# Fused attention and two MoE layers: unread products in early PE gaps, three key tiles in the accumulator, GpSimd taken from the first splits, an early sigmoid table, new order constants

## The chip, the cores and the metric

One core of a Trainium2 chip. The metric is the device time of the whole program in microseconds (us), median of several runs. The names used are those of the profile: PE is TensorE, DVE VectorE, ACT ScalarE, POOL GpSimd, SP the engine whose queue issues DMAs.

## The reference

```
scores = q k^T / 8, kept where the key is one of 4 sinks or within a window of 128, else -1e9
a = softmax(scores); x = (a v), heads put side by side          # 2 x 768 tokens, 8 heads of 64, so 1536 x 512
h = x @ w_in; g = h if h >= 1, 0 if h <= -1, else (h + 1)^2 / 4; x = g @ w_out          # d_ff 2048
gate = sigmoid(x @ w_gate); val = x @ w_val; out = (gate * val) @ w_out2                # d_ff 1536
```

The weights are float64 in memory and are passed as pairs of 32-bit words.

## The kernel before, in words

**Attention.** Each of the two batches is cut in seven query tiles of 112 tokens (the last has 96), numbered t = 0 to 13 over both; each tile has four head pairs. For a pair: PE multiplies queries and keys (scores, L873, 64 rows of the array at a time), DVE scales, masks and takes the extreme of a row (`top`, L876, two for a pair), ACT takes the exponential and sums (L882), PE transposes (L890), ACT or DVE copies the transposes out of PSUM (`pts`), PE multiplies by the values (L913, 64 columns at a time, the four pairs of a tile together). At a tile's end the sums are inverted (L927, L928, DVE), widened to `ie`, spread by four transposes (L936), and the output `on` is copied, multiplied (L947) and split in two fp32r parts, `xh` (a copy) and `xl` (a difference).

**MoE.** Every product runs on such split parts, three matmuls for one (L515 to L517 for w_in, L560 to L562 for w_out, L671 for the gate and value layer, which forms blocks from seven products of sums). The first block of 512 tokens can start when the first five tiles (t = 0 to 4) are split. Weights are decoded from float64 words: a DMA into `st`, then `rebase` on ACT (L418), `clamp` and `shift` (L421, L424), `sign` and `tail` (L427, L430) on DVE, then `halves` splits the result into the tiles `early` or `late`: a copy (L324, L326 or L328 on ACT, DVE or POOL) and a difference (L331 on DVE or POOL).

**The order.** Nothing runs in the order of the code. Every piece is given to `Plan.op` with its engine or the engines it may go to, a cost for each, a due time and what it reads and writes. `Plan.order` walks through time with these costs, picks for each free engine the piece that is due first (`SAME_MODE` prefers, on PE, the mode of 64 rows, 64 columns or the full array that it is in), and chooses engine and PSUM bank; the instructions are issued in that order. Each engine, and SP's queue of DMAs, then runs its list in order and waits on semaphores. The constants at the file's head (`FINISH`, `EARLY`, `LATE`, `BIAS`, ...) move due times.

**The start.** Before a branch that tests the sizes, keys and queries of tile 0 are loaded into the then unused accumulator `acc`, its values behind them, both from SP; six unread matmuls run on PE (L1158). Keys of later tiles go to `qk` buffers with two places for each pair; an even and an odd tile lie side by side, which is why tile 1 needs tile 0's block loaded a second time.

Of the kernel before, what the change touches and what calls it, by code (L numbers as in the profile page):

```python
# [54 lines left out]
BIAS = {"DVE": 0.02, "POOL": -0.14, "ACT": -0.17}  # L55

SLOT_DUE = 2.54

FINISH = {"top": 1.49, "exp": 7.0, "turn": 1.26, "pts": 2.81, "values": -0.74, "div": 3.95, "out": 4.29}
MOE_DUE = 63.45  # L60
MOE_PACE = 3.48
DRAIN = 3.77
EARLY = 11.77
LATE = 18.92
# [5 lines left out]
SAME_MODE = 1.11  # L70
WARM = 6

# [9 lines left out]
def a_us(n):  # L82
    return 0.093 + n / 1200
# [14 lines left out]
def g2_us(n):  # L98
    return 0.15 + n / 476
# [34 lines left out]
class Plan:  # L134
# [130 lines left out]
    def run(self):  # L265
        order, end = self.order()
        for o in order:
            for b in o.new:
                b.ap = b.ring.make(b.bank if b.ring.banks else b.at % b.ring.n)
            o.fn(o.eng) if o.pick else o.fn()  # L270
        return end


class Body:
# [46 lines left out]

    def copy(self, e, out, x):
# [53 lines left out]
    def halves(self, x, n, hi, lo, hk, lk, due, reads, after=()):  # L376
# [27 lines left out]
    def raw(self, src, due):  # L404
# [12 lines left out]
        def rebase():  # L417
            nc.scalar.activation(out=w.ap, in_=high().bitcast(F32), func=AF.Copy, scale=REBASE)  # L418
# [14 lines left out]
        op("ACT", a_us(512), due, rebase, [st], [w])  # L433
# [6 lines left out]
    def load(self, nm, i, due):  # L440
# [8 lines left out]
        def split(x, c, n, reads):  # L449
            self.halves(x, n, lambda: self.at(h, c, n), lambda: self.at(l, c, n), self.held(h, c, n), self.held(l, c, n), due, reads, after)  # L450
# [138 lines left out]


# [191 lines left out]
    def moe(self, first):  # L782

        rest = []
# [11 lines left out]
    def banded(self):  # L796
# [25 lines left out]
        def slot(k, due):  # L822
# [3 lines left out]
            mask = masks.of(i)  # L826

            ks = 1 if i == 0 else 2
            at = i % 2
# [5 lines left out]
            src = lambda j: self.a["qk"][b, j, p]  # L835
            if t == 0:
                c0, *there = pre["raw"][p]
                own, v = (lambda: there[0]), (lambda: there[1])
                rq, rv = cells("acc", 0, c0, c0 + NQK), cells("acc", 0, c0 + NQK, c0 + NQK + P)
                op("SP", 0.0, -99.0, lambda: None, [], rq, lat=0.0)  # L840
                op("SP", 0.0, -99.0, lambda: None, [], rv, lat=2.0 + 0.2 * p)
            else:
                v_b = Buf(v_r)
                own, v = (lambda: block(p, at)), (lambda: v_b.ap)
                rq, rv = [mine, before] if i else [mine], [v_b]
# [12 lines left out]
            def keys(es):  # L858

                x = kept[p][es]  # L860
                if at:
# [58 lines left out]
            if p == NP - 1:  # L920
# [23 lines left out]
                op({"ACT": a_us(NP * P), "DVE": d1_us(NP * P), "POOL": g1_us(NP * P)}, 0, due - FINISH["div"], widen, [sm], [ie])  # L944
# [3 lines left out]
                op({"ACT": a_us(m), "DVE": d1_us(m), "POOL": g1_us(m)}, 0, due - FINISH["out"], lambda e: self.copy(e, xh, y()), [on], xhk)  # L948
                self.att_end = op({"DVE": d2_us(m), "POOL": g2_us(m)}, 0, due - FINISH["out"], lambda e: self.less(e, xl, y(), f32v(xh)), [on] + xhk, xlk)
# [119 lines left out]
class Masks:  # L1069
# [20 lines left out]
    def of(self, i):  # L1090
        return (self.first, self.second, self.even, self.odd)[min(i, 2 + i % 2)]
# [28 lines left out]
def moe_chain_kernel(ctx: ExitStack, tc: tile.TileContext, a, out):  # L1120
# [12 lines left out]
    with tc.manual_schedule():  # L1133
# [5 lines left out]
        for p in range(min(KD, NP)):  # L1139
            c0 = p * NT + S  # L1140
            qk = pre["acc"][:, c0:c0 + NQK]
# [98 lines left out]
```

## Time and profile before

| | |
|---|---|
| time, median of 3 runs | 641.52 us (641.24 to 641.83) |
| time of the profiled execution | 640.57 us |
| its span, first to last instruction | 638.8 us |
| PE busy, share of the span | 624.0 us, 98% |
| DVE, ACT, POOL busy | 518.8, 316.2, 81.8 us |
| TensorE clock, mean granted | 0.994 |
| PE busy before 52.1 us, where the first MoE product starts | 44.17 us |
| PE idle in 345 to 372 us | 1.50 us |
| PE idle in 625 to 638.8 us | 5.40 us |

Idle time before the first MoE product (7.93 us), in the one gap near 370 us and at the end make up nearly all that PE is not busy in. A busy PE can still be at half clock.

### The profile page before, as it was taken

How to read it: one execution, taken by the hardware profiler on the slowest of the kernel's cores; microseconds unless marked ns; L12 is line 12 of the kernel's file. 1: busy time of each engine (PE TensorE's matmuls, PEld its weight loads, DVE VectorE, ACT ScalarE, POOL GpSimd, SP SyncE). 2: the span in 40 equal slices, each digit the busy share in tenths (PEclk: the TensorE clock that was granted, in tenths of full speed). 3: DMA queues.
4: the chain of work that ended last, by engine and by line, in shares of the span. 5: the costliest groups of instructions: out<-in, count | busy, mean ns of one | idle time of the engine just before them, and what ended most of it. 6: DMA issues, size and time to landing. Idle time of an engine off the chain costs nothing.

```text
span 638.8 us, 9816 instructions
## 1 busy us (share of the span) xinstructions
PE 624.0 (98%) x3514; PEld 540.4 (85%) x3514; DVE 518.8 (81%) x1136; ACT 316.2 (50%) x723; POOL 81.8 (13%) x95
## 2 busy tenths in 40 slices
PE   8979999999999999999999999999999999999996
PEld 5667788888888888888888889999999998999995
DVE  4899999699999885456979598799887899786373
ACT  4989988655533521232535376554352353433330
POOL 0022200020100120010102111122120021120000
PEclk8999999999999999999999999999999999999999
DMA  6666665122534130000310003322211222200004
GB/s 189 208 199 207 202 188 197 51 72 94 165 107 129 62 99 34 0 1 13 120 34 1 1 0 100 100 66 67 72 61 34 100 94 72 67 0 1 2 34 170
DMA packets 28571, 54.48 MB, mean 85 GB/s; under 512 B 3296, under 2 KB 18400, under 8 KB 28512
## 3 DMA queue, kind: packets, MB, share of 16 engines
q1 hardware_dynamic: 28512, 53.75, 25.8%
q8 instruction: 30, 0.49, 0.3%
q14 instruction: 29, 0.24, 0.1%
HBM read 50.60 MB, written 3.15 MB: 84 GB/s over the span
## 4 chain that ended last, share of the span: by engine, by line
PE 92%; DVE 3%; ACT 3%; issue 0%; DMA 0%; POOL 0%; DVEq 0%; ACTq 0%
PE bank L671 27%; PE bank L515 7%; PE bank L560 7%; PE bank L517 7%; PE bank L516 7%; PE bank L562 7%; PE bank L561 7%; PE bank L758 5%; PE bank L759 5%; PE bank L757 5%; PE bank L873 3%; PE bank L913 3%; PE bank L890 2%; DVE pr L876 1%; ACT pr L882 1%; PE bank L936 1%
## 5 line engine op out<-in xcount | busy, mean ns | idle before, releaser
L671 PE MATMUL bank<-xh,early 128*128 128x384 f32 x384 | 107.7, 335 | 1.5 <-ACT bank L324 1.5
L671 PE MATMUL bank<-late,early 128*128 128x384 f32 x432 | 85.2, 335 | 0.0
L671 PEld LDWEIGHTS bank<-late,early 128*128 128x128 f32 x432 | 76.0, 188 | 0.6
L671 PEld LDWEIGHTS bank<-xh,early 128*128 128x128 f32 x384 | 70.2, 188 | 2.4 <-ACT bank L324 2.1
L324 ACT ACTIVATE early<-w 128x512 fp32r<-128x512 f32 (+1 forms) x46 | 26.2, 572 | 86.0 <-PE bank L671 32.9
L671 PE MATMUL bank<-xl,early 128*128 128x384 f32 x192 | 64.3, 335 | 0.0
L767 DVE TENSOR_TENSOR acc<-bank,acc 128x512 f32<-128x512 f32 (+1 forms) x61 | 41.4, 679 | 26.4 <-PE bank L759 26.3
L882 ACT ACTIVATE pr<-pr,mx 112x256 f32<-112x256 f32 (+2 forms) x112 | 54.0, 488 | 9.3 <-DVE mx L876 9.0
L418 ACT ACTIVATE w<-st 128x512 f32<-128x512 f32 x68 | 44.9, 668 | 15.2 <-DMA st<-in_w 9.4
L534 ACT ACTIVATE tmp<-tmp 128x512 f32<-128x512 f32 x48 | 30.1, 630 | 42.8 <-DVE tmp L531 42.5
L427 DVE SCALAR_TENSOR_TENSOR w<-st,w 128x512 int32<-128x512 int32 x68 | 46.8, 691 | 0.5
L430 DVE SCALAR_TENSOR_TENSOR w<-st,w 128x512 int32<-128x512 int32 x68 | 46.7, 689 | 0.4
L531 DVE TENSOR_SCALAR tmp<-bank 128x512 f32<-128x512 f32 x48 | 32.7, 685 | 17.1 <-PE bank L517 16.8
L576 DVE TENSOR_TENSOR acc<-bank,acc 128x512 f32<-128x512 f32 x36 | 24.1, 687 | 23.5 <-PE bank L562 23.4
L876 DVE CUSTOM_DVE_ANT_0 pr<-bank,mask 112x256 f32<-112x256 f32 (+2 forms) x112 | 39.4, 394 | 4.5 <-PE bank L873 4.5
L324 ACT ACTIVATE gs<-tmp 128x512 fp32r<-128x512 f32 (+1 forms) x49 | 30.4, 621 | 23.6 <-DVE tmp L537 21.7
L331 DVE TENSOR_TENSOR gs<-tmp,gs 128x512 fp32r<-128x512 f32 (+1 forms) x51 | 34.4, 678 | 5.5 <-ACT gs L324 5.0
L515 PE MATMUL bank<-xh,early 128*128 128x512 f32 x96 | 38.8, 404 | 0.0
L560 PE MATMUL bank<-gs,early 128*128 128x512 f32 x96 | 38.2, 398 | 0.0
L517 PE MATMUL bank<-xh,early 128*128 128x512 f32 x96 | 37.5, 391 | 0.0
L516 PE MATMUL bank<-xl,early 128*128 128x512 f32 x96 | 37.5, 390 | 0.0
L562 PE MATMUL bank<-gs,early 128*128 128x512 f32 x96 | 37.4, 390 | 0.0
(170 smaller groups left out, 1498.3 us busy)
## 6 DMA issues: line engine op xcount, KB each, us to landing
st<-in_w SPq DMA_DIRECT2D x32, 512.0 KB, 3.4
qk<-in_qk SPq DMA_DIRECT2D x56, 128.0 KB, 3.0
v<-in_vb SPq DMA_DIRECT2D x52, 128.0 KB, 3.3
st<-in_wg SPq DMA_DIRECT2D x12, 512.0 KB, 3.3
st<-in_wv SPq DMA_DIRECT2D x12, 512.0 KB, 3.3
st<-in_wo SPq DMA_DIRECT2D x12, 512.0 KB, 3.3
out<-acc SPq DMA_DIRECT2D x11, 256.0 KB, 2.3
acc<-in_qk SPq DMA_DIRECT2D x4, 128.0 KB, 2.8
```

Source lines behind the costliest of these rows:

```text
L324: self.nc.scalar.activation(out=out, in_=x, func=AF.Copy)
L418: nc.scalar.activation(out=w.ap, in_=high().bitcast(F32), func=AF.Copy, scale=REBASE)
L427: nc.vector.scalar_tensor_tensor(out=t(), in0=high(), scalar=-0x80000000, in1=t(), op0=ALU.bitwise_and, op1=ALU.bitwise_or)
L430: nc.vector.scalar_tensor_tensor(out=t(), in0=low(), scalar=29, in1=t(), op0=ALU.logical_shift_right, op1=ALU.bitwise_or)
L515: mm(out=out, lhsT=wh[:, c], rhs=mh, start=k == 0, stop=False)
L516: mm(out=out, lhsT=wh[:, c], rhs=ml, start=False, stop=False)
L517: mm(out=out, lhsT=wl[:, c], rhs=mh, start=False, stop=k == KD - 1)
L560: mm(out=out, lhsT=wh[:, c], rhs=gh, start=f == fs[0], stop=False)
L562: mm(out=out, lhsT=wl[:, c], rhs=gh, start=False, stop=f == fs[-1])
L671: nc.tensor.matmul(out=out, lhsT=w[:, c], rhs=m, start=start and i == n == 0, stop=i == 1 and n == 2, skip_group_check=True)
L876: nc.vector.tensor_tensor_reduce(out=pr.ap[:n, e, :ks * P], in0=banks[e].ap[:n, j, :ks * P], in1=mask[:n, :ks * P], op0=ALU.add, op1=ALU.m ...
L882: nc.scalar.activation(out=pr.ap[:n, e, :ks * P], in_=pr.ap[:n, e, :ks * P], func=AF.Exp, bias=mx.ap[:n, e:e + 1], scale=-1.0, accum_out=s ...
```

## The change

- `fillers` and `fill`: where the plan leaves PE idle for more than 0.32 (in the plan's units) in the first 55, fp32 products of the 128 x 128 identity by itself are put in, into a PSUM bank that is free then; nobody reads them.
- `RAW` = 3: keys and queries of the tiles 0, 1 and 2 lie in `acc`, side by side, so the block of tile 0 isn't loaded again for tile 1; the `qk` buffers begin at tile 3, where tile 2's block is loaded a second time. The values of tile 0 are loaded from ACT's queue.
- `some`, `pool`, `POOL_FROM` = 5: the splits of the first eight weight pieces, and for the tiles 0 to 4 `widen` and the split of the output, may no longer go to POOL.
- `raw`: `rebase` of the first eight weight pieces may go to POOL as well as to ACT.
- `table`: a sigmoid of one element on ACT behind the attention's last split.
- Constants of the order, `SAME_MODE` from 1.11 to 3.41 among them.

```diff
-FINISH = {"top": 1.49, "exp": 7.0, "turn": 1.26, "pts": 2.81, "values": -0.74, "div": 3.95, "out": 4.29}
+FINISH = {"top": 0.74, "exp": 7.79, "turn": 6.83, "pts": 5.29, "values": -2.39, "div": 3.03, "out": -3.93}
...
-SAME_MODE = 1.11
+SAME_MODE = 3.41
 WARM = 6
+RAW = 3
+POOL_FROM = 5
+FILL, FILL_US, FILL_MIN = 55.0, 0.22, 0.1
...
+    def fillers(self, order, banks):
+        spans = [[] for _ in banks]
+        for b in {b for o in self.ops for b in o.bufs if b.bank is not None}:
+            spans[b.bank].append((min(u.start for u in b.users), max(u.end for u in b.users)))
+        todo, last = {}, 0.0
+        for o in order:
+            if o.eng != "PE":
+                continue
+            n = int((o.start - last - FILL_MIN) / FILL_US)
+            if o.start < FILL and n > 0:
+                free = [i for i, s in enumerate(spans) if all(z < last or a > o.start for a, z in s)]
+                if free:
+                    todo[o] = n, free[0]
+            last = o.start + o.on["PE"]
+        return todo
...
+    def fill(self, n, bank):
+        for _ in range(n):
+            self.nc.tensor.matmul(out=self.psum[bank][:, :P], lhsT=self.pre["ident"], rhs=self.pre["ident"], start=True, stop=True)
...
+    def some(self, pool, **on):
+        return {e: t for e, t in on.items() if pool or e != "POOL"}
...
-        hp = self.plan.op({"ACT": a_us(n), "DVE": d1_us(n), "POOL": g1_us(n)}, 0, due, lambda e: self.copy(e, hi(), x()), reads, hk, after=after)
-        lp = self.plan.op({"DVE": d2_us(n), "POOL": g2_us(n)}, 0, due, lambda e: self.less(e, lo(), x(), f32v(hi())), [*reads, *hk], lk, after=after)
+        hp = self.plan.op(self.some(pool, ACT=a_us(n), DVE=d1_us(n), POOL=g1_us(n)), 0, due, lambda e: self.copy(e, hi(), x()), reads, hk, after=after, port=True)
+        lp = self.plan.op(self.some(pool, DVE=d2_us(n), POOL=g2_us(n)), 0, due, lambda e: self.less(e, lo(), x(), f32v(hi())), [*reads, *hk], lk, after=after, port=True)
...
-        op("ACT", a_us(512), due, rebase, [st], [w])
+        op({"ACT": a_us(512), "POOL": g1_us(512)} if self.asked < 2 * STAGES[0] else {"ACT": a_us(512)}, 0, due, rebase, [st], [w])
...
+        x = self.pre["scratch"]
+        self.plan.op("ACT", 1.5, self.due, lambda: self.nc.scalar.activation(out=x, in_=x, func=AF.Sigmoid), after=[self.att_end])
...
+            if t < RAW:
+                c0, first = pre["raw"][p]
+                held = lambda j: cells("acc", 0, c0 + j * NQK, c0 + (j + 1) * NQK)
+                own = lambda: pre["acc"][:, c0 + t * NQK:c0 + (t + 1) * NQK]
+                rq = [k for j in (t - 1, t) if j >= 0 for k in held(j)]
+            else:
+                own, rq = (lambda: block(p, at)), [mine, before] if i else [mine]
...
-                if t == 1:
-                    load(lambda: block(p, 0), src(0), due - 6, [before])
-                load(own, src(i), due - 6, [mine])
+                if t == RAW:
+                    load(lambda: block(p, 1 - at), src(i - 1), due - 6, [before])
+                load(own, src(i), due - 6, held(t) if t < RAW else [mine])
...
-                op({"ACT": a_us(NP * P), "DVE": d1_us(NP * P), "POOL": g1_us(NP * P)}, 0, due - FINISH["div"], widen, [sm], [ie])
+                pool = t >= POOL_FROM
+                op(self.some(pool, ACT=a_us(NP * P), DVE=d1_us(NP * P), POOL=g1_us(NP * P)), 0, due - FINISH["div"], widen, [sm], [ie], port=True)
...
-            nc.sync.dma_start(out=v, in_=a["vb"][0, 0, p, :, 1])
+            nc.scalar.dma_start(out=v, in_=a["vb"][0, 0, p, :, 1])
```

What this makes of the order is shown at three places. Names: `bank` is a PSUM bank, `pr` the exponentials, `ident` the identity, `st` and `w` a weight as loaded and as decoded.

PE between the scores of tile 0 and the values of tile 0, before:

```order
L890 MATMUL bank_164<-ident,pr 128x112 x2
L890 MATMUL bank_165<-ident,pr 128x112 x2
L873 MATMUL bank_158<-qk_175 112x256
L873 MATMUL bank_159<-qk_175 112x256
L873 MATMUL bank_158<-qk_179 112x256
L873 MATMUL bank_159<-qk_179 112x256
L936 MATMUL bank_162<-ident,ie 128x112 x4
L913 MATMUL bank_160<-pts,acc 64x112 x8
```

and of the change (L349 is a product that nobody reads, L922 scores, L939 transposes):

```order
L349 MATMUL bank_163<-ident 128x128 x5
L939 MATMUL bank_162<-ident,pr 128x112 x2
L349 MATMUL bank_158<-ident 128x128
L939 MATMUL bank_163<-ident,pr 128x112 x2
L349 MATMUL bank_158<-ident 128x128 x4
L922 MATMUL bank_164<-acc 112x256
L922 MATMUL bank_165<-acc 112x256
L922 MATMUL bank_164<-acc 112x256
L922 MATMUL bank_165<-acc 112x256
L939 MATMUL bank_158<-ident,pr 128x112 x2
L939 MATMUL bank_159<-ident,pr 128x112 x2
L349 MATMUL bank_161<-ident 128x128 x2
```

Ten unread products now stand ahead of tile 1's first scores, those scores have moved ahead of the last two pairs' transposes of tile 0, and they read `acc`. Up to the first MoE product there are 29 such products. The last scores of tile 2 stand behind the spread of tile 1 before, and ahead of it in the change.

POOL from the branch on, before:

```order
L328 TENSOR_SCALAR xh<-on 128x4x112 x2
L328 TENSOR_SCALAR early<-w 128x512
L328 TENSOR_SCALAR ie<-sm 112x512
L331 TENSOR_TENSOR early<-w,early 128x512 x2
L328 TENSOR_SCALAR ie<-sm 112x512 x2
L328 TENSOR_SCALAR early<-w 128x512
L331 TENSOR_TENSOR early<-w,early 128x512
L331 TENSOR_TENSOR xl<-on,xh 128x4x112
```

and of the change (L453 is `rebase`, L357 a copy, L360 a difference):

```order
L453 TENSOR_SCALAR w<-st 128x512 x4
L357 TENSOR_SCALAR ie<-sm 112x512
L453 TENSOR_SCALAR w<-st 128x512 x2
L357 TENSOR_SCALAR xh<-on 128x4x112
L453 TENSOR_SCALAR w<-st 128x512 x2
L360 TENSOR_TENSOR gs<-tmp,gs 128x512
L357 TENSOR_SCALAR ie<-sm 112x512
L360 TENSOR_TENSOR xl<-on,xh 128x4x112
```

All eight rebases have gone to POOL, and the differences that stood third on its list have gone to DVE.

ACT where the first gates are formed, before:

```order
L324 ACTIVATE gs<-w 128x512
L324 ACTIVATE tmp<-bank_165 128x384
L324 ACTIVATE late<-acc 128x384
L712 ACT_TABLE_LOAD
L712 ACTIVATE rest<-bank_158 128x384
L324 ACTIVATE xh<-rest 128x384
L324 ACTIVATE late<-tmp 128x384
L324 ACTIVATE bank_161<-bank_160 128x384
```

and of the change:

```order
L353 ACTIVATE late<-acc 128x384
L451 ACTIVATE w<-st 128x512
L353 ACTIVATE xh<-rest 128x384
L753 ACTIVATE rest<-bank_164 128x384
L353 ACTIVATE tmp<-bank_165 128x384
L353 ACTIVATE bank_160<-bank_158 128x384
```

The load of the sigmoid's table (L712 before) is no longer among these; it stands behind the attention's last split on ACT's list.

## Rows read from the trace of the kernel before

**Rows 1.** The page: PE's busy time, and its clock in 40 slices.

```profile
PE 624.0 (98%) x3514; PEld 540.4 (85%) x3514; DVE 518.8 (81%) x1136; ACT 316.2 (50%) x723; POOL 81.8 (13%) x95
...
PEclk8999999999999999999999999999999999999999
```

**Rows 2.** Stretches: PE, PEld, DVE, ACT, POOL busy; PE clock, DMA share, GB/s.

```profile
0.00:52.10 52.10, 44.17 (x380) 32.19 (x381) 41.45 (x167) 39.32 (x130) 7.70 (x21) 0.93 0.63 198
...
52.10:130.00 77.90, 77.90 (x688) 63.29 (x687) 71.35 (x232) 65.82 (x199) 8.66 (x11) 1.00 0.52 163
...
9.90:16.30 6.40, 6.40 (x36) 4.23 (x36) 2.79 (x14) 3.20 (x11) 0.00 (x0) 0.50 0.84 252
...
37.00:46.00 9.00, 6.26 (x66) 4.58 (x66) 8.90 (x31) 6.62 (x22) 1.58 (x2) 1.00 0.65 228
```

**Rows 3.** Who waited for whom: us in total, times, longest.

```profile
PE bank L936 <- POOL ie L328: 2.1, 3, 1.4
...
PE bank L671 <- ACT bank L324: 1.5, 1, 1.5
...
ACT pr L882 <- DVE mx L876: 9.0, 4, 4.6
```

**Rows 4.** Timeline of DVE: start, us, instruction, idle before it and its releaser.

```profile
12.73 0.42 DVE L876 CUSTOM_DVE_ANT_0 pr<-bank,mask 112x256 f32<-112x256 f32 x1 [1.58 <-PE bank L873]
...
15.95 0.62 DVE L947 TENSOR_TENSOR on<-on,bank 128x448 f32<-128x448 f32 x1 [1.76 <-ACT on L324]
...
17.62 0.42 DVE L876 CUSTOM_DVE_ANT_0 pr<-bank,mask 112x256 f32<-112x256 f32 x1 [0.51 <-PE bank L873]
...
23.52 0.42 DVE L876 CUSTOM_DVE_ANT_0 pr<-bank,mask 112x256 f32<-112x256 f32 x1 [1.74 <-PE bank L873]
...
24.90 0.76 DVE L421 TENSOR_SCALAR w<-w 128x512 f32<-128x512 f32 x2
...
34.95 3.50 DVE L331 TENSOR_TENSOR xl<-on,xh 128x448 fp32r<-128x448 f32 x1
...
44.51 0.72 DVE L331 TENSOR_TENSOR xl<-on,xh 128x448 fp32r<-128x448 f32 x1
```

**Rows 5.** Timeline of POOL.

```profile
35.47 2.49 POOL L331 TENSOR_TENSOR early<-w,early 128x512 fp32r<-128x512 f32 x2
44.13 0.62 POOL L328 TENSOR_SCALAR ie<-sm 112x512 f32<-112x512 f32 x1 [6.17 <-DVE sm L928]
```

**Rows 6.** The chain that ended last: start, us, engine, tile, line.

```profile
18.05 0.54 DVE xl L331
...
28.39 0.34 DVE ie L326
...
40.01 0.54 DVE pts L326
...
41.23 0.34 DVE pr L876
...
63.15 1.05 PE bank L873 x8
...
81.65 1.91 PE bank L873 x16
```

**Rows 7.** Timeline of PE: the unread products before the branch.

```profile
1.73 2.93 PE L1158 MATMUL warm<-ident 128*128 128x128 f32 x12 [1.73 <-POOL ident masks.py:199]
```

**Rows 8.** SP's queue, and DMA issues of the first 20 us with time to landing.

```profile
13.57 0.90 SPq L415 DMA_DIRECT2D st<-in_w  x2
...
st<-in_w SPq DMA_DIRECT2D x3, 512.0 KB, 4.8
```

**Rows 9.** Timeline of ACT, and of PE, at the first gates.

```profile
367.74 1.28 ACT L712 ACT_TABLE_LOAD   x1
369.04 0.49 ACT L712 ACTIVATE rest<-bank 128x384 f32<-128x384 f32 x1
...
370.79 0.44 PE L671 MATMUL bank<-xh,early 128*128 128x384 f32 x1 [1.50 <-ACT bank L324]
```

More of the change, by code (lines that the diff above doesn't have):

```diff
@@ L53 @@
 START = {"DVE": 0.9}
-BIAS = {"DVE": 0.02, "POOL": -0.14, "ACT": -0.17}
-SLOT_DUE = 2.54
-FINISH = {"top": 1.49, "exp": 7.0, "turn": 1.26, "pts": 2.81, "values": -0.74, "div": 3.95, "out": 4.29}
[L60 to L64, printed above, removed]
+BIAS = {"DVE": 0.32, "POOL": -0.16, "ACT": -0.15}
+SLOT_DUE = 2.58
+FINISH = {"top": 0.74, "exp": 7.79, "turn": 6.83, "pts": 5.29, "values": -2.39, "div": 3.03, "out": -3.93}
+MOE_DUE = 65.99
+MOE_PACE = 3.5
+DRAIN = 2.46
+EARLY = 10.7
+LATE = 23.51
 ENTER, LEAVE = {"rows": 0.18, "cols": 0.14}, 0.09
@@ L263, in order, with run @@
         return order, now
-    def run(self):
+    def fillers(self, order, banks):
[13 more added lines that the diff above has]
+        return todo
+    def run(self, banks=(), fill=None):
         order, end = self.order()
+        todo = self.fillers(order, banks) if fill else {}
         for o in order:
+            if o in todo:
+                fill(*todo[o])
             for b in o.new:
@@ L415, in dma, with rebase @@
             nc.sync.dma_start(out=st.ap.rearrange("p n t -> p (n t)"), in_=src.bitcast(I32))
-        def rebase():
-            nc.scalar.activation(out=w.ap, in_=high().bitcast(F32), func=AF.Copy, scale=REBASE)
+        def rebase(e):
+            if e == "ACT":
+                nc.scalar.activation(out=w.ap, in_=high().bitcast(F32), func=AF.Copy, scale=REBASE)
+            else:
+                nc.gpsimd.tensor_scalar(out=w.ap, in0=high().bitcast(F32), scalar1=REBASE, scalar2=1.0, op0=ALU.mult, op1=ALU.mult)
         def clamp():
@@ L449, in split @@
         def split(x, c, n, reads):
-            self.halves(x, n, lambda: self.at(h, c, n), lambda: self.at(l, c, n), self.held(h, c, n), self.held(l, c, n), due, reads, after)
+            self.halves(x, n, lambda: self.at(h, c, n), lambda: self.at(l, c, n), self.held(h, c, n), self.held(l, c, n), due, reads, after, self.asked >= 2 * STAGES[0])
         if nm not in PAIR_AT:
@@ L588, in block, with table @@
         after(3, t)
+    def table(self):
+        x = self.pre["scratch"]
+        self.plan.op("ACT", 1.5, self.due, lambda: self.nc.scalar.activation(out=x, in_=x, func=AF.Sigmoid), after=[self.att_end])
     def quarters(self, b):
@@ L782, in moe @@
     def moe(self, first):
+        if first:
+            self.table()
         rest = []
@@ L947, in slot @@
                 op("DVE", d2_us(m), due - FINISH["div"], lambda: nc.vector.tensor_tensor(out=y(), in0=y(), in1=ib.ap[:, :, :n], op=ALU.mult), [ib], [on])
-                op({"ACT": a_us(m), "DVE": d1_us(m), "POOL": g1_us(m)}, 0, due - FINISH["out"], lambda e: self.copy(e, xh, y()), [on], xhk)
-                self.att_end = op({"DVE": d2_us(m), "POOL": g2_us(m)}, 0, due - FINISH["out"], lambda e: self.less(e, xl, y(), f32v(xh)), [on] + xhk, xlk)
+                op(self.some(pool, ACT=a_us(m), DVE=d1_us(m), POOL=g1_us(m)), 0, due - FINISH["out"], lambda e: self.copy(e, xh, y()), [on], xhk, port=True)
+                self.att_end = op(self.some(pool, DVE=d2_us(m), POOL=g2_us(m)), 0, due - FINISH["out"], lambda e: self.less(e, xl, y(), f32v(xh)), [on] + xhk, xlk, port=True)
             yield None
@@ L1166, in moe_chain_kernel @@
             body.moe(1)
-            body.plan.run()
+            body.plan.run(body.banks, body.fill)
     with branch.Else():
```

33 lines of the change are left out of this document (16 added, 17 removed).

## The prediction

> **What bounds the kernel now.** I read the page first. PE is busy for 98% of the span and its clock is full in 39 of 40 slices [rows 1], so time can come back only where PE stands, where its clock is low, or where its list gets shorter. The table of stretches finds these places: up to 52.1 us, where the first MoE product starts, PE is busy for 44.17 us, so it stands 7.93; from there to 130 us it is busy throughout [rows 2]. The waits add one place, 1.5 us behind ACT at the first gates [rows 3, 9]. The rest of PE's idle time lies at the end (front table), which the change doesn't touch. So the end comes when the first MoE product starts, plus what PE's list then takes: a microsecond that the first five tiles gain early is a microsecond of the total, as long as PE stays full afterwards.
>
> What holds the first product back, then? Three things. From 9.9 to 16.3 us PE is busy all the time at a clock of 0.50 [rows 2], the lower of its two levels, 1.2 GHz; before that it had stood between short transposes. DVE waits in this stretch and behind it four times, 1.58, 1.76, 0.51 and 1.74 us [rows 4]. And at 34.95 us a difference that usually delays the next DVE instruction by 0.54 [rows 6] takes 3.50 [rows 4], while GpSimd works on two differences for 2.49 [rows 5]; around it PE is busy for only 6.26 us of 9.00 and DVE for 8.90 [rows 2]. From about 25 us on DVE is full, and what its list holds up to tile 4's split decides.
>
> **The change part by part.** The profiled execution took 640.57 us, 0.95 below the median of 641.52; the sum is made against 640.57 and carried over to the median. A difference of under 0.2%, 1.28 us, is about what this measurement cannot tell from none.
>
> *Unread products.* Six of them took 2.93 us before the branch [rows 7], at the low clock by my reading, 0.49 each; half of it, 0.24, at the high one. Ten of them stand between tile 0's scores and tile 1's, 2.4 us in a place where PE only had four pairs of transposes and waited for exponentials. If that keeps the clock up, the 6.40 us of work at 0.50 [rows 2] take 3.2: a gain of 3.2, taken out of DVE's first three waits, which sum to 3.85 [rows 4]. Bounds: 0, if the clock falls anyway, and 3.85. I take 3.2, since DVE stood exactly behind PE's slow scores and values. One product stands ahead of tile 0's scores: +0.49 at the low clock (bounds 0 and 0.49). The 17 later ones lie in gaps of the plan; where a gap is not there they cost 17 x 0.24 = 4.1, which is the far bound; I take 0, because PE has idle time of 2.74 us in 37 to 46 alone [rows 2] and DVE, not PE, is behind.
>
> *The order of scores.* The fourth wait of 1.74 is for scores of tile 2 that stood on PE's list behind a spread, which itself waited for DVE. They now stand ahead of the spread: -1.74 (bounds 0 and -1.74).
>
> *Keys in the accumulator.* Tile 1 needs four loads fewer, but the queue of SP now issues the keys of tile 3, twice the count for that tile, ahead of the first weights: the first `st` is the 23rd DMA behind the branch instead of the 17th. It was issued at 13.57, two issues take 0.90, so six more put it at about 16.3, and with 4.8 us to landing [rows 8] it is there at 21.1. GpSimd's rebase takes 0.62, by the copy of 512 elements for each partition in rows 5: ready at 21.7. DVE came to its first clamp at 24.90 [rows 4]; less the 4.9 of waits, with the 0.49, and 0.2 for a reshuffled list (four more `top`, less three copies, by the 0.34 and 0.54 of [rows 6]) it comes at 20.7. So it now waits 1.0 there, and behind the clamp on DVE's list queue the last `top` of tile 3 and the division of tile 1, for which ACT and PE wait. Bounds: 0 and 2.2 (a landing one microsecond later). The four loads of tile 0's values sit on ACT's list ahead of its first table load; ACT waits up to 4.6 us for its first exponential [rows 3], which covers four issues of 0.45. Without that cover they would cost 1.8.
>
> *First splits without GpSimd.* The stall goes: 3.50 - 0.54 = -2.96. DVE's list up to the fifth `xl` changes, counted in the two orders: one cast of a weight and one of `xh` more (0.34 and about 0.30), two differences of weights more (0.54 for 448 elements gives 0.62 for 512, so 1.24), four `top` of tile 5 more (4 x 0.34 = 1.36), and six `pts` copies fewer, two of them half as wide (4 x 0.54 + 2 x 0.27 = 2.70): +0.54. The rebases go off ACT, which is busy for 39.32 of 52.1 us [rows 2] and so not first in line; it takes over the copies and two widenings.
>
> *What the sum doesn't see.* DVE, ACT and PE now all end their lists for tile 4 within a few microseconds of each other, and small waits between them remain. Bounds 0 and 2.74, PE's idle time in 37 to 46 [rows 2]; I take 1.0, below the middle, because in that stretch DVE was busy for 8.90 of 9.00.
>
> So the first product starts at 52.1 - 3.2 + 0.49 - 1.74 + 1.0 - 2.96 + 0.54 + 1.0 = 47.2, 4.9 us earlier.
>
> *After it.* PE's groups of scores behind the first product fall from ten to seven. Two groups apart cost 2 x 1.05, together 1.91 [rows 6]: 0.19 for each, -0.57 (bounds 0 and -0.57). DVE is busy for 71.35 of 77.9 us up to 130 and ACT for 65.82 [rows 2], so the table load of 1.28, now at the attention's end, has 12 us of ACT's idle time to lie in, and costs nothing; if PE had to wait for it there, 1.28. Five differences of `xl` go to GpSimd behind the first product: nothing, or some stalls as below.
>
> *The gates.* ACT loads the sigmoid's table for 1.28 us in front of the first gate, and PE waits 1.50 for a copy that stands behind it [rows 9]. Without the load the copy comes 1.28 earlier: -1.28 (bounds 0, if the new list of ACT, which puts a rebase there, is as late, and -1.50). By the Trainium skill, ScalarE: Activation LUTs, "What ACT_TABLE_LOAD costs", a change of set costs a drain of about 1.38 us beside the 1.28, 2.66 in all. The trace agrees with the 1.28; the next sigmoid starts 0.02 us behind the load [rows 9], so no drain shows behind it, and by the page the gain would still be no more than the 1.50 that PE waits.
>
> Sum: -4.9 - 0.57 - 1.28 = -6.8, or 633.8 for the profiled execution and **634.7** for the median.
>
> **The rivals.** *GpSimd holds DVE again.* The stalled difference of 3.50 [rows 4] shows that DVE can be held for as long as GpSimd works. Five rebases of 0.62 each run before the first product now; if each holds a DVE instruction for its whole time, that is 3.1, and the time 637.8. Against it: beside a copy of 0.62 on GpSimd at 44.13 [rows 5] the difference at 44.51 took 0.72 [rows 4], longer by 0.1 to 0.2 and not 0.62, and before the change there were about as many such copies in this stretch. The Trainium skill, GPSIMD Engine Reference, "Key points", says that GpSimd shares its SBUF interfaces with VectorE, with contention where a VectorE instruction runs in a 2-port mode or has two SBUF inputs. The 3.50 agrees with it, and the clamp, shift and sign behind each rebase are instructions of these kinds.
>
> *The clock falls all the same.* Then DVE's first three waits stay (3.2 of them were counted as gained), and the twelve unread products up to tile 1's last scores take 0.49, not 0.24: of these 12 x 0.25 = 3.0 I count half, as PE has gaps there. 634.7 + 3.2 + 1.5 = 639.4. For it: which stretches are granted the full clock isn't something that the list alone decides. Against it: PE has hardly a gap from 5 to 12 us in the new list.
>
> *The earlier start is lost again.* The DVE that is busy for 92% of 52 to 130 us becomes what PE waits for, and the seven microseconds go in one- and two-microsecond waits: 641.5, no change. Against it: PE waited not once in that stretch, and DVE gives work to GpSimd there.
>
> *Slower: weights behind keys.* The clamp of the first weight stands on DVE's list ahead of everything that tile 3's end needs. If its DMA, behind six more loads, lands late, all tops behind it wait, microsecond for microsecond. The forecast has it at 21.1; the gain of 6.8 is used up at 27.9 and the time is worse by 0.2% from 29.2 on, at some 642.9. Against it: three such DMAs landed within about 4.8 us with the engines near full [rows 8].
>
> *More than that.* No wait at the clamp, no friction, the wait at the gates gone whole: 634.7 - 1.0 - 1.0 - 0.2 = 632.5, and a further one if PE's list packs better.
>
> **How the numbers follow.** Forecast 0.58, its own range 633.2 to 636.8 (friction and the clamp's wait at their bounds). GpSimd 0.15, the clock 0.10, no gain 0.06, slower 0.05, more 0.06. The range of 632.0 to 639.4 takes in the forecast, GpSimd, half of the clock and most of "more": 0.83. Faster by over 0.2%: 0.58 + 0.15 + 0.06 and most of the clock, 0.09, 0.88; the same 0.07; slower 0.05.
>
> **What would show it.** The clock at 1.00 from about 7 us on; no DVE difference above 1 us before the first product; that product at 46 to 48.5 us; a wait of DVE for POOL at its first clamp near 21 us; no wait of PE above 0.5 us at the first gates; PE full between. It would be wrong by its first step if PE's clock shows 0.50 between 10 and 17 us, by its last if PE's list, once full, shows new waits after 50 us.

## The result and the profile after

The changed kernel takes **634.27 us** (median of 4 runs, 632.1 to 634.69) against 641.67 (641.24 to 642.7) for the kernel before: ratio 0.9883, 95% interval 0.9869 to 0.9898. The forecast was 634.7. The profiled execution after took 633.94 with a span of 632.1. So the total came as forecast; whether it came from where the forecast said is what the rest is about.

The page of the kernel after, beside [rows 1]: PE's busy time is the same to half a microsecond, but the span is shorter by 6.6, so PE's idle time fell from 14.8 to 8.6. Of the 623.5 us, 10.4 are unread products behind the branch, of which the kernel before has none. GpSimd does twice as much.

```profile
PE 623.5 (99%) x3572; PEld 546.2 (86%) x3572; DVE 498.3 (79%) x1026; ACT 322.2 (51%) x742; POOL 168.7 (27%) x187
...
PEclk9999999999999999999999999999999999999999
```

The same stretches as in [rows 2], with a last one at the first gates:

```profile
0.00:52.10 52.10, 48.86 (x486) 41.35 (x488) 42.83 (x189) 43.82 (x150) 6.62 (x20) 1.00 0.72 223
...
9.90:16.30 6.40, 6.40 (x62) 5.04 (x61) 3.84 (x23) 5.62 (x24) 0.00 (x0) 1.00 0.84 244
37.00:46.00 9.00, 8.04 (x93) 6.72 (x92) 8.97 (x31) 8.34 (x28) 0.00 (x0) 1.00 0.73 221
...
345.00:372.00 27.00, 27.00 (x142) 25.06 (x141) 19.30 (x34) 14.26 (x32) 7.42 (x8) 1.00 0.00 1
```

The clock from 9.9 to 16.3 us is now 1.00 where it was 0.50. PE stands 1.0 of the 9.0 us where it stood 2.74, and not at all at the gates. Its waits, all that are left (the first, for the identity ahead of the warm-up, was there before):

```profile
PE warm L1206 <- POOL ident masks.py:199: 1.7, 1, 1.7
PE bank L349 <- DVE mx L925: 1.0, 1, 1.0
PE bank L349 <- DVE mask L1149: 0.5, 1, 0.5
PE bank L595 <- DVE mx L925: 0.3, 1, 0.3
```

L349 is an unread product, so two of the other three are unread products that had to wait themselves.

The first MoE product and the last product of PE, timeline of the kernel after:

```profile
48.40 0.48 PE L550 MATMUL bank<-xh,early 128*128 128x512 f32 x1
...
626.72 0.28 PE L800 MATMUL bank<-gs,early 128*128 128x256 f32 x1
```

and the last product of the kernel before:

```profile
633.12 0.28 PE L759 MATMUL bank<-gs,early 128*128 128x256 f32 x1
```

With these the 6.6 us of span split up: the first MoE product starts 3.7 earlier (52.1 to 48.4, forecast 4.9); from it to the last product PE takes 578.6 for 581.3, 2.7 less (forecast 0.57 + 1.28 = 1.85), of which 1.5 is the wait at the gates [rows 9]; the last 0.2 is the tail.

The opening, step by step. Timeline of PE after:

```profile
5.15 0.76 PE L349 MATMUL bank<-ident 128*128 128x128 f32 x2 [0.50 <-DVE mask L1149]
5.85 2.05 PE L922 MATMUL bank<-acc 64*112 64x128 f32 x16
7.83 2.15 PE L349 MATMUL bank<-ident 128*128 128x128 f32 x10
...
10.44 1.07 PE L349 MATMUL bank<-ident 128*128 128x128 f32 x8
```

A product here has two records. Ten records took 2.15 us at 7.83, eight took 1.07 at 10.44: 0.22 against 0.13 each. So tile 0's scores and the first unread products still ran at the lower rate. The rows of the granted clock begin only at 9.47 us in this execution, with 1.00; ahead of its first row a view prints 1.00 too, so there the lengths of the products have to be read instead.

Timeline of DVE after, beside [rows 4]: its waits from 12 to 30 us, the first clamp, and the longest `xl` ahead of the first MoE product.

```profile
12.37 0.17 DVE L976 TENSOR_SCALAR sm<-sm 112x8 f32<-112x8 f32 x1 [1.77 <-ACT pr L931]
...
14.64 0.42 DVE L925 CUSTOM_DVE_ANT_0 pr<-bank,mask 112x256 f32<-112x256 f32 x1 [0.53 <-PE bank L922]
...
16.85 0.62 DVE L997 TENSOR_TENSOR on<-on,bank 128x448 f32<-128x448 f32 x1 [0.74 <-ACT on L353]
...
17.67 0.42 DVE L925 CUSTOM_DVE_ANT_0 pr<-bank,mask 112x256 f32<-112x256 f32 x1 [0.20 <-PE bank L922]
...
22.92 0.55 DVE L456 TENSOR_SCALAR w<-w 128x512 f32<-128x512 f32 x1
...
25.11 0.42 DVE L925 CUSTOM_DVE_ANT_0 pr<-bank,mask 112x256 f32<-112x256 f32 x1 [0.45 <-PE bank L922]
...
33.92 0.96 DVE L360 TENSOR_TENSOR xl<-on,xh 128x448 fp32r<-128x448 f32 x1
```

In place of the four waits of [rows 4], 5.59 together, stand four of 1.92 and one of 1.77 ahead of them, at 12.37, behind ACT's exponentials of tile 0. Up to the clamp they sum to 3.24. The wait of 1.74 for tile 2's scores is gone; the 0.45 at 25.11 is for those of a later tile. The `xl` of 3.50 is gone. The clamp waits for nothing, at 22.92. The first weights' loads on SP's queue, and the first rebase on GpSimd:

```profile
16.14 0.91 SPq L447 DMA_DIRECT2D st<-in_w  x2
```

```profile
21.20 0.68 POOL L453 TENSOR_SCALAR w<-st 128x512 f32<-128x512 f32 x1 [18.96 <-DMA st<-in_w]
...
33.72 0.68 POOL L453 TENSOR_SCALAR w<-st 128x512 f32<-128x512 f32 x1 [6.76 <-DMA st<-in_w]
```

The forecast had the first two at 16.3 and 21.1. The third line, a later rebase, stands beside the `xl` of 0.96.

### The profile page after: what moved, and what is told of

Read it like the earlier page. It is cut to its first block, busy times and chain, and to the rows that moved or that the text cites. A ratio compares the mean times of both kernels' runs of the same rounds, so it can differ in the third digit from the quotient of the medians.

```text
span 632.1 us, 9945 instructions
## 1 busy us (share of the span) xinstructions
PE 623.5 (99%) x3572; PEld 546.2 (86%) x3572; DVE 498.3 (79%) x1026; ACT 322.2 (51%) x742; POOL 168.7 (27%) x187
## 4 chain that ended last, share of the span: by engine, by line
PE 88%; DVE 10%; DMA 0%; issue 0%; DVEq 0%
PE bank L712 28%; PE bank L595 7%; PE bank L597 7%; PE bank L596 7%; PE bank L550 6%; PE bank L552 6%; PE bank L551 6%; PE bank L800 5%; PE bank L799 5%; PE bank L798 5%; DVE pr L925 3%; PE bank L922 2%; PE bank L962 1%; PE bank L939 1%; DVE w L465 1%; PE bank L349 1%
## 5 line engine op out<-in xcount | busy, mean ns | idle before, releaser
L712 PE MATMUL bank<-xh,early 128*128 128x384 f32 x384 | 107.7, 335 | 0.0
L712 PE MATMUL bank<-late,early 128*128 128x384 f32 x432 | 85.1, 334 | 0.0
L712 PEld LDWEIGHTS bank<-late,early 128*128 128x128 f32 x432 | 76.0, 188 | 0.5
L712 PEld LDWEIGHTS bank<-xh,early 128*128 128x128 f32 x384 | 70.3, 188 | 0.4
L712 PE MATMUL bank<-xl,early 128*128 128x384 f32 x192 | 64.2, 334 | 0.0
L808 DVE TENSOR_TENSOR acc<-bank,acc 128x512 f32<-128x512 f32 (+1 forms) x61 | 41.5, 681 | 22.4 <-PE bank L800 21.9
L353 ACT ACTIVATE early<-w 128x512 fp32r<-128x512 f32 (+1 forms) x48 | 27.7, 579 | 58.7 <-PE bank L800 28.1
L465 DVE SCALAR_TENSOR_TENSOR w<-st,w 128x512 int32<-128x512 int32 x68 | 51.5, 758 | 0.7
L360 POOL TENSOR_TENSOR early<-w,early 128x512 fp32r<-128x512 f32 (+1 forms) x29 | 35.0, 1208 | 63.2 <-ACT early L353 50.8
L451 ACT ACTIVATE w<-st 128x512 f32<-128x512 f32 x60 | 39.7, 665 | 17.6 <-DVE gs L360 7.0
L462 DVE SCALAR_TENSOR_TENSOR w<-st,w 128x512 int32<-128x512 int32 x68 | 48.0, 707 | 0.6
L405 POOL TENSOR_TENSOR w<-w 128x256 f32<-128x256 f32 x48 | 43.3, 912 | 18.1 <-DVE w L465 9.2
L925 DVE CUSTOM_DVE_ANT_0 pr<-bank,mask 112x256 f32<-112x256 f32 (+2 forms) x112 | 38.1, 396 | 2.4 <-PE bank L922 2.4
L550 PE MATMUL bank<-xh,early 128*128 128x512 f32 x96 | 38.5, 401 | 0.0
L595 PE MATMUL bank<-gs,early 128*128 128x512 f32 x96 | 38.1, 397 | 0.3 <-DVE mx L925 0.3
L360 DVE TENSOR_TENSOR early<-w,early 128x512 fp32r<-128x512 f32 x41 | 33.0, 806 | 6.8 <-POOL early L357 6.3
L456 DVE TENSOR_SCALAR w<-w 128x512 f32<-128x512 f32 x68 | 34.7, 513 | 4.6 <-ACT w L451 4.6
```

What stands on the lines that cost most here:

```text
L353: self.nc.scalar.activation(out=out, in_=x, func=AF.Copy)
L462: nc.vector.scalar_tensor_tensor(out=t(), in0=high(), scalar=-0x80000000, in1=t(), op0=ALU.bitwise_and, op1=ALU.bitwise_or)
L465: nc.vector.scalar_tensor_tensor(out=t(), in0=low(), scalar=29, in1=t(), op0=ALU.logical_shift_right, op1=ALU.bitwise_or)
L550: mm(out=out, lhsT=wh[:, c], rhs=mh, start=k == 0, stop=False)
L595: mm(out=out, lhsT=wh[:, c], rhs=gh, start=f == fs[0], stop=False)
L712: nc.tensor.matmul(out=out, lhsT=w[:, c], rhs=m, start=start and i == n == 0, stop=i == 1 and n == 2, skip_group_check=True)
```

## The experiments

The theory to test was the forecast's: every part brings its own term. The rival was that the planner's new numbers bring the time by another order, whatever the parts do. Twelve kernels, each in five rounds beside the kernel before. *First* is the start of the first MoE product in the one execution that was profiled, *the list behind it* the time from there to the end of PE's last product. The medians of the kernel before were 641.08 to 641.67, so differences of a few tenths between two rows of the table say nothing.

| kernel | median us (lowest to highest) | before, same runs | ratio, 95% | first |
|---|---|---|---|---|
| after | 634.27 (632.1 to 634.69) | 641.67 | 0.9883 (0.9869 to 0.9898) | 48.40 |
| *after, one part back* | | | | |
| no unread products | 634.63 (633.71 to 635.02) | 641.08 | 0.9893 (0.9877 to 0.9908) | 49.42 |
| late unread products out | 634.05 (633.66 to 634.87) | 641.53 | 0.9874 (0.9853 to 0.9896) | 49.37 |
| table at the gates | 634.4 (634.09 to 635.31) | 641.08 | 0.9899 (0.9883 to 0.9914) | 48.81 |
| GpSimd on first splits | 634.95 (633.2 to 636.4) | 641.08 | 0.9903 (0.9886 to 0.9919) | 48.09 |
| charge of 1.11 | 635.31 (633.76 to 636.13) | 641.53 | 0.9893 (0.9871 to 0.9914) | 47.87 |
| all numbers of before | 637.88 (636.11 to 638.32) | 641.25 | 0.9947 (0.9931 to 0.9963) | 47.97 |
| keys of one tile | 638.21 (636.11 to 638.91) | 641.25 | 0.9950 (0.9933 to 0.9967) | 50.97 |
| *before, with a part* | | | | |
| GpSimd off first splits | 641.47 (640.72 to 642.87) | 641.08 | 1.0006 (0.9996 to 1.0015) | 50.44 |
| unread products | 639.6 (638.27 to 641.72) | 641.25 | 0.9973 (0.9959 to 0.9986) | 53.10 |
| new numbers | 638.56 (638.38 to 638.94) | 641.25 | 0.9963 (0.9948 to 0.9977) | 51.07 |
| keys of three tiles | 637.94 (637.1 to 638.76) | 641.53 | 0.9934 (0.9913 to 0.9955) | 48.89 |
| keys and new numbers | 637.63 (637.14 to 639.04) | 641.53 | 0.9936 (0.9916 to 0.9957) | 49.48 |

**No unread products** (the order of after, without them):

```diff
-            body.plan.run(body.banks, body.fill)
+            body.plan.run()
```

> The changed kernel with the same order on all engines, but without the 29 unread products ahead of the first MoE product. If they hold the clock (the prediction's step): PE at 0.50 again for some 5 to 7 us between 9 and 18 us, the first product 1.5 to 3 us later than the 48.4 of the changed kernel, time 636 to 637.5. If they only stand in the way: clock as in the changed kernel, the first product up to 1 us earlier, time 633.3 to 634.3.

634.63: 0.4 us lost, within the intervals. The products do hold the clock; these stretches of that kernel were granted half of it:

```profile
9.20:12.60 3.40, 3.40 (x18) 2.11 (x16) 2.43 (x15) 2.92 (x14) 0.00 (x0) 0.50 0.88 256
43.40:46.70 3.30, 3.30 (x34) 2.91 (x32) 3.30 (x9) 2.44 (x10) 0.00 (x0) 0.50 0.55 192
```

That is 6.7 us at the low clock, and it costs 1.0 us of the profiled span (633.1 for 632.1) and 0.4 between the medians. Why so little: in this kernel ACT is busy for 9.89 of the 10 us from 15 to 25 and DVE for 9.93 of those from 25 to 35, PE for 9.04 and 8.40. So I take it that most of what PE loses at the low clock it would have waited anyway; that is an argument from these rows, not a run.

**Late unread products out** (those up to 16 us of the plan stay, 15 of the 29, so that 14 are left out and not the 18 of the expectation):

```diff
-FILL, FILL_US, FILL_MIN = 55.0, 0.22, 0.1
+FILL, FILL_US, FILL_MIN = 16.0, 0.22, 0.1
```

> The kernel after with the unread products of the first 16 us of the plan alone, the 18 later ones left out; the same order else. If the later ones only lie in gaps, as the forecast had it: 634.0 to 634.8. If they hold PE up (one waited 1.0 us for DVE at 41.5 us): 633.0 to 633.8. If they keep the clock up where it fell from 43.3 to 46.7 us without any of them: 634.8 to 636.

634.05, the same as after: the late ones cost nothing and bring nothing. Without them the clock is at 0.50 from 43.8 to 47.2 us and the first product of the profiled execution 1.0 later, but that does not show between the medians.

**Unread products alone**, added to the kernel before:

```diff
+FILL, FILL_US, FILL_MIN = 55.0, 0.22, 0.1
-            body.plan.run()
+            body.plan.run(body.banks, body.fill)
```

> The kernel before with unread products in the planned waits of PE up to 55 us, and nothing else. By the forecast's term (all of the stretch at clock 0.50 comes back, and DVE's first waits with it): 3.2 us, 638.3. By what the kernel after loses without them: 0.4 to 1.0 us, 640.2 to 640.8. If an earlier first MoE product isn't carried to the end in the order of before, as when GpSimd was taken off the first splits: 641 to 641.8 with the first product 1 to 3 us earlier.

639.6, a gain of 1.7 in medians (the interval is 0.9 to 2.6): half of the 3.2. The execution that was profiled took 641.48, one of the three longest of twelve, and shows no gain; so its rows show what can be lost, and not where the 1.7 come from. The longest of PE's waits there:

```profile
PE bank L347 <- DVE mx L903: 2.5, 1, 2.5
```

L347 is an unread product; at 38.64 it has waited 2.5 us for DVE to have read the bank it was given. DVE was late because the stall of [rows 4] is here again, beside the same two differences, and behind PE's wait the clock fell:

```profile
34.75 3.49 DVE L358 TENSOR_TENSOR xl<-on,xh 128x448 fp32r<-128x448 f32 x1
```

```profile
35.27 2.49 POOL L358 TENSOR_TENSOR early<-w,early 128x512 fp32r<-128x512 f32 x2
```

```profile
40.30:43.60 3.30, 3.30 (x28) 2.69 (x26) 3.20 (x13) 2.86 (x10) 0.00 (x0) 0.50 0.56 152
```

The nine executions of this kernel with a mean clock of 0.999 or 1.000 took 638.3 to 640.7; the three others, this one among them, 641.4 to 641.7. The wait of 1.74 for tile 2's scores [rows 4] is still 1.74 here, though the clock is full: it belongs to the order, as the forecast had it.

**Table at the gates** (order of after; the early activation loads no new table, so the first sigmoid does):

```diff
-... activation(out=x, in_=x, func=AF.Sigmoid), after=[self.att_end])
+... activation(out=x, in_=x, func=AF.Copy), after=[self.att_end])
```

> The changed kernel with the same order, but the one-element activation at the attention's end is a copy, so the sigmoid's table is loaded at the first gate. If the load caused the wait at the gates: PE waits 1.0 to 1.5 us there again, time 635.3 to 635.8. If ACT's new order alone took the wait away: no such wait, 634.3.

634.4: nothing lost. The load stands in front of the gates again, and PE waits for nothing there. Timeline of its ACT:

```profile
362.12 1.28 ACT L753 ACT_TABLE_LOAD   x1
```

The load comes 5.6 us earlier than in [rows 9]; PE's own list is 4.3 earlier at that layer's first product (342.34 for 346.64). So the load has moved by about 1.3 against PE's list, and ACT's list around it is another. With the numbers of before and the table at the attention's end ("all numbers of before") PE still waits there:

```profile
PE bank L712 <- ACT bank L353: 0.9, 1, 0.9
```

So the wait at the gates is a matter of the order that the numbers give, and the load by itself worth little: with the old numbers, moving it away leaves 0.9 of the 1.5.

**GpSimd on first splits** again (after, planned anew; the rebases stay on GpSimd):

```diff
-POOL_FROM = 5
+POOL_FROM = 0
-... due, reads, after, self.asked >= 2 * STAGES[0])
+... due, reads, after)
```

> The changed kernel with GpSimd allowed again in all splits and widenings, order planned anew. If keeping GpSimd out of the first splits is worth what the prediction's term says (2.96): a DVE difference of 2 us or more before the first product, that product 1.5 to 3 us later, 636 to 637.3. If the 3.50 was the accident of one order: no such difference, 634 to 635.

634.95: 0.7 more, the intervals overlap. Up to the first product one `xl` took 1.02 and none 3.50.

**GpSimd off first splits**, alone, in the kernel before: `POOL_FROM = 5` and the same argument of `split`, nothing else.

> The kernel before with nothing changed but that GpSimd may not take the splits of the first eight weight pieces and of the first five tiles. By the prediction's term: no DVE difference above 1 us before 52 us, first product at 49 to 50.5, time 638.7 to 640.2. If the work that goes back to DVE and ACT costs as much as the stall: 641 to 642.5.

641.47: no gain. The stall went (no `xl` over 0.63 before the first product) and the first product came 1.7 earlier; but from there to the last product PE took 585.0 us for 581.3. The order has 24 groups of scores for 20, and PE's waits behind the first product were now these, where before there was the 1.5 at the gates alone:

```profile
PE bank L675 <- ACT bank L325: 1.5, 1, 1.5
PE bank L894 <- ACT pr L886: 1.1, 1, 1.1
PE bank L520 <- DVE xl L332: 0.4, 1, 0.4
```

These are 1.5 us of the 3.7 that the list is longer; in the other 2.2 PE is busy. Four groups of scores at the forecast's 0.19 would be 0.8 of them; the rest stays open. An earlier first product is thus not carried to the end by itself.

**New numbers** in the kernel before: the constants from `BIAS` to `LATE`, and `SAME_MODE`.

> The kernel before with nothing but the new numbers of the planner (biases, finish times, due times, the charge for a change of kind from 1.11 to 3.41); no new function, no unread product, keys of one tile in the accumulator, GpSimd allowed everywhere, table at the first gate. Theory that the numbers carry the change: most of the 7.3 us come, 634.5 to 638, PE's wait at the gates is gone although the table still loads there, and PE's list behind the first MoE product is shorter than the 586.7 us of before. Rival, that the parts carry it (each by its term in the forecast): no gain, 640 to 642.5, a wait of 1 to 2 us at the gates stays.

638.56, a gain of 2.7, between the two. The wait at the gates is gone, with the table's load still in front of them (366.57).

**All numbers of before** in the kernel after.

> The kernel after with the planner's numbers of before; unread products, keys of three tiles, the exclusion of GpSimd and the table at the attention's end stay. Theory that the numbers carry the change: most of the gain goes, 638 to 641.5. Rival, that the parts carry it: 633.5 to 636.5, since the terms of the forecast that belong to parts sum to 5 to 6 us.

637.88, a loss of 3.6, just under what the theory of the numbers had (638) and clear of the rival's 636.5. The first product is *earlier* than in the kernel after, 47.97; the list behind it is 3.8 longer (582.4 for 578.6), with 22 groups of scores for 16 and the wait of 0.9 at the gates.

**Charge of 1.11**: of these numbers only the one for a change of kind on PE.

```diff
-SAME_MODE = 3.41
+SAME_MODE = 1.11
```

> The kernel after with one number of before: the planner's charge for a change of kind on PE, 1.11 and not 3.41. PE's list then has 21 groups of scores and not 16. If this one number is what the new numbers are worth (taken out together they cost 3.5 us): 637 to 638.5. If each group of scores costs only the 0.19 that the forecast charged: 634.4 + 5 x 0.19 = 635.3. If other numbers carry it: 634.4 to 634.8.

635.31. Counted in the orders, PE's list has 20 groups of scores before, 16 after and 21 here; the loss of 1.0 is 0.21 for each of the five, the forecast's 0.19. The interval reaches down to no loss, so the size is only borne out, not settled. In the profiled execution the list is 1.5 longer, or 0.3 for each, and the first product 0.5 earlier.

**Keys of one tile** in the accumulator, rest as after:

```diff
-RAW = 3
+RAW = 1
```

> The kernel after with the keys of tile 0 alone in the accumulator, as before the change. If the keys of three tiles are only the wait at the first clamp that the forecast charged (1.0 us, which the trace after doesn't show), the time stays within 0.6 us of 634.4. If they matter because they make the first groups of scores independent of keys loaded for each tile, the first MoE product comes 1 to 2 us later and the time is 635.5 to 636.5. If the queue of loads was the price, it is 633 to 634.

638.21: 3.9 us lost, more than any of the three expectations. In the profiled execution the first product is 2.6 later, and the list behind it 1.5 longer, with 21 groups of scores for 16. **Keys of three tiles** alone is the other side: the kernel after with the numbers of before, no unread products, rebases on ACT, GpSimd on all splits, table at the gates; tile 0's values stay on ACT's queue.

> Only the keys of three tiles in the accumulator, with the planner's numbers of before; 21 groups of scores. If keys and numbers add up (numbers alone gave 2.7 us, both without the rest 5 to 7): 637 to 639. If the keys help only where the numbers let the planner use them: 640.5 to 642. If the forecast's price for them is all there is (a wait at the first clamp): 641.5 to 642.5.

637.94, a gain of 3.6 (the interval is 2.9 to 5.6). So the part that the forecast charged with +1.0 is the largest single gain of those tried, though its interval overlaps that of the numbers alone (1.5 to 3.3). SP's queue shows what it changes. Whom it waited for longest from 4 to 30 us in the kernel before:

```profile
SPq L832 <- PE bank L873: 6.5, 4, 2.6
```

and its loads of keys there (start, length from the first issue of a row to the end of its last):

```profile
17.20 0.80 SPq L832 DMA_DIRECT2D qk<-in_qk  x2
...
18.81 5.09 SPq L832 DMA_DIRECT2D qk<-in_qk  x4
```

and the loads with three tiles' keys in the accumulator:

```profile
11.79 3.91 SPq L872 DMA_DIRECT2D qk<-in_qk  x8
15.75 1.38 SPq L447 DMA_DIRECT2D st<-in_w  x3
```

Before, the keys of the tiles 2 and 3 went into `qk` blocks that an earlier tile's scores still read: SP waited 6.5 us for PE's scores, in four waits, and the last keys of tile 3 were issued at 23.55 and landed at 25.6. With the accumulator as a second place, all eight loads that tile 3 needs go out by 15.7 and have landed by 18.8. PE has done tile 3's scores by 25.1 there, and by 28.7 before. The queue as a whole doesn't wait less:

```profile
SPq L872 <- PE bank L960: 9.1, 5, 5.0
SPq L872 <- PE bank L920: 2.7, 5, 1.3
```

but these waits stand behind tile 3's keys and three weights, and not ahead of them. In the kernel with one tile's keys the last two pairs are late again:

```profile
19.24 1.41 SPq L874 DMA_DIRECT2D qk<-in_qk  x2
...
25.32 0.80 SPq L874 DMA_DIRECT2D qk<-in_qk  x2
```

and landed at 27.8. What the traces of these kernels don't show is an engine that waits long for these loads: up to 30 us there is one wait of 0.3, of PE's weight load in the kernel before. The plan counts with the time at which a load can go out, and places the scores by it. So that keys in the accumulator bring the time is shown from both sides; that they do so through this queue is read from the rows and not shown by a run.

**Keys and new numbers**: the same kernel with the new numbers. It differs from the kernel after in four parts, each nearly free when taken out alone, or not tried alone: unread products, table, GpSimd on the first splits, and rebases, which are ACT's here.

> Of the change only the keys of three tiles in the accumulator (with tile 0's values on ACT's list of loads) and the planner's new numbers; no unread product, GpSimd allowed on all splits and off the rebases, the sigmoid's table at the first gate. PE's list has 20 groups of scores, as before the change; the kernel after has 16. Theory that keys and numbers together carry the change and the other parts are worth next to nothing, as each was when taken out alone: 634.5 to 636. Rival, that the other parts only show together: 637 to 639, no better than the numbers alone at 638.6.

637.63: the rival's number; beside the keys the new numbers bring 0.3, which is nothing measurable. The stretches show a difference on DVE. Keys and new numbers, PE, PEld, DVE, ACT, POOL:

```profile
16.00:24.00 8.00, 7.85 (x86) 5.92 (x84) 5.40 (x28) 7.93 (x29) 2.33 (x3) 1.00 0.85 282
24.00:32.00 8.00, 8.00 (x91) 6.73 (x90) 5.43 (x28) 8.00 (x29) 1.76 (x3) 1.00 0.77 233
32.00:40.00 8.00, 6.71 (x77) 5.28 (x76) 5.93 (x28) 8.00 (x28) 1.18 (x2) 1.00 0.67 186
```

and the kernel "GpSimd on first splits", which differs from it by rebases on GpSimd, unread products and the table alone:

```profile
16.00:24.00 8.00, 8.00 (x90) 6.35 (x91) 6.52 (x34) 7.93 (x27) 3.68 (x5) 1.00 0.78 247
24.00:32.00 8.00, 8.00 (x96) 6.81 (x94) 7.66 (x27) 8.00 (x29) 1.97 (x3) 1.00 0.54 170
32.00:40.00 8.00, 8.00 (x91) 6.63 (x88) 7.93 (x29) 7.91 (x28) 5.03 (x6) 1.00 0.69 227
```

ACT is full in both. With the rebases on its list, DVE stands for almost a third of the time; with them on GpSimd it is nearly full from 24 us on. The reason isn't that the rebases fill ACT, but that a full ACT gets to them late: before its first product this kernel has rebased one weight, the other five. And PE waits for what becomes of that weight and of later ones; from the first product on:

```profile
PE bank L550 <- POOL early L357: 1.3, 1, 1.3
PE bank L597 <- POOL early L360: 0.9, 1, 0.9
PE bank L595 <- POOL early L357: 0.7, 1, 0.7
```

The first of these is the first MoE product itself. Its weight was rebased here, the only one so far:

```profile
44.45 0.72 ACT L451 ACTIVATE w<-st 128x512 f32<-128x512 f32 x1
```

Then come DVE's four steps, and the copy on GpSimd ends at 49.43; the product starts at 49.48. "GpSimd on first splits" has none of these 2.9 us of waits, though GpSimd may take the same splits there. The two kernels are 2.7 us apart; unread products (0.4 by their removal) and table (0.1) leave some 2.2, about the size of these waits. That the rebases are these 2.2 is still worked out from differences and rows; a kernel with the rebases alone put back was not run.

## Why the prediction was right

The total was right, and some of its steps, but the sum came out through errors of opposite sign: that it came within half a microsecond is luck.

**Right, as to place and size.** The full clock from 9.9 to 16.3 us, though it came only at about 9.5 and not at 7. No stall of `xl`, the longest 0.96. The load of the first weights, to within 0.2 us. The groups of scores at 0.19 each, about 0.21 measured. No wait at the gates. Tile 2's scores ahead of the spread: DVE's wait of 1.74 for them is gone, and it stayed 1.74 where only unread products were added. An early start that is lost again, the rival of 641.5, did not come; "GpSimd off first splits" shows that it was real in the order of before.

**Right in mechanism, wrong in size: unread products.** The step "I take 3.2, since DVE stood exactly behind PE's slow scores and values" took a clock's gain for the path's. Taken out they cost 0.4; added alone they bring 1.7. Tile 0's scores start 0.92 later than before (5.85 for 4.93) and still run slowly; DVE's three waits shrank, but one of 1.77 came ahead of them, so that in place of their 3.85 stand 3.24, 0.6 less and not 3.2. The "+0.49" for the product ahead of the scores was too small, as it had to wait 0.50 for a mask besides.

**Wrong: "Keys in the accumulator", +1.0.** The step counted what the six more loads delay and not what they release. The loads of the tiles 2 and 3 had waited in SP's queue for PE's scores, 6.5 us in all; the forecast read that queue for the weights' issue alone. The wait at the clamp that it expected didn't come either: the rebase ended at 21.9, forecast 21.7, but DVE was there only at 22.92, forecast 20.7, as its waits up to there fell by 2.35 and not by 4.9. (In that step "four more `top`, less three copies" is -0.26 by its own rows and not +0.2; at half a microsecond it decides nothing. And with friction and the clamp's wait at their stated bounds the range would be 632.7 to 637.6 and not 633.2 to 636.8.) In place of +1.0 stand -3.6 (alone) or -3.9 (taken out). Some of the step "the order of scores", -1.74, may sit in it, since tile 2's keys lie in the accumulator too; it was not tried alone.

**Wrong as a term of its own: "First splits without GpSimd", -2.96.** The stall was real and went, but the exclusion brings nothing alone, and little is lost without it. Alone it brought the first product 1.7 forward and made the list behind it 3.7 longer, 1.5 of it in waits for ACT and DVE. Nor was it needed: in the four kernels with GpSimd allowed and another order, the longest `xl` was 0.71 to 1.36.

**Wrong: the rebases "go off ACT ... and so not first in line", at nothing.** ACT's 39.32 of 52.1 us [rows 2] were an average over a stretch in which it was full from 25 to 35:

```profile
25.00:35.00 10.00, 9.92 (x104) 7.65 (x100) 9.93 (x38) 9.99 (x35) 1.41 (x3) 1.00 0.61 178
```

Under the new numbers, with the rebases still there, ACT is full from 16 us on, the weights are decoded late, and PE waits 2.9 us for their splits. By the differences above taking them off is worth about 2.2.

**Wrong as to cause: the table, -1.28.** The wait of 1.50 at the gates is gone, but it is gone with the load in front of the gates too, in "table at the gates" and in "new numbers", and not gone (0.9) with the load moved and the old numbers. The order does most of it.

**Friction, +1.0**, can't be told apart from what the other terms were off by: the first product came at 48.4, 1.2 later than the sum's 47.2, and the list behind it made up for 0.85 of it.

The parts don't add up in any case. Alone, keys, numbers, unread products and exclusion bring 3.6, 2.7, 1.7 and nothing; keys and numbers together 3.9. Both the theory and its rival fall in their pure form: the keys bring half, and beside them the numbers paid 3.6 with the rebases off ACT and 0.3 with the rebases on it. What exactly joins keys, numbers and rebases to 7.4 beyond that stays open. No version beat the changed kernel by more than the measurement can tell.

## What to carry to other kernels

When a load is issued earlier or into another buffer, look at what its queue waited for before: a load that stood behind a buffer's release can be worth more than all that it pushes back. An engine's busy share over a stretch says little about who is first in line; cut it finer, and look again under the new assignment. And a gain at the start of a full engine's list is only kept if the order behind it still fits: check the first product and the list behind it as two numbers.

## What the runs showed of the hardware

- Unread products were not the only way to the full clock. The kernel with keys and new numbers has none behind the branch, and from its first row, at 13.1 us, it was granted 1.00 and no 0.50 before PE's end; the kernel before had 0.50 from 9.9 to 16.3. Up to about 13 us it ran at the lower rate all the same, as eight records of scores show, 2.05 us against 1.12 for the same shape later:

```profile
9.14 2.05 PE L920 MATMUL bank<-acc 64*112 64x256 f32 x8
...
15.58 1.12 PE L920 MATMUL bank<-acc 64*112 64x256 f32 x8
```

- An `xl` beside a rebase of 0.68 on GpSimd took 0.96 instead of 0.62, longer by half of that rebase; the 3.50 beside two differences of 2.49 came back, as 3.49, in "unread products", the one kernel that keeps the order of before. In the twelve kernels with another order, with GpSimd's differences there or not, the longest `xl` on DVE before the first product was 1.36 ("keys of three tiles").
- A product whose result nobody reads still waits for its bank: 1.0 us in the kernel after, 2.5 in the kernel before with them added, where 3.3 us at 0.50 followed.
